# Sixty tasks of a written-out order moved ahead of the key sums, and four halves of query features swapped between VectorE and GpSimd

## The chip, the cores and the metric

The kernel runs on one core of a Trainium2 chip. The time is the device time of one execution in microseconds (us), and the median of the runs is what counts. A profiled execution has its own time and a span, from its first to its last instruction; the places below are given in us from the start of that span.

## The reference

The input x has 2048 tokens of 512 features. A small network on a vector c gives six vectors of 512 (shift, scale and gate for each of two branches). The first branch is linear attention with 32 heads of 16 features, the second a gated feed-forward network of width 1376:

```python
mod = (_silu(c) @ w_mod).reshape(c.shape[0], 6, 1, -1)
h = _layernorm(x) * (1 + ca) + sa
qkv = h @ wqkv                       # q, k, v per head
pq, pk = q @ w_phi, k @ w_phi        # per head, 16 x 16
phi_q = concat([softmax(pq), softmax(-pq)]); phi_k likewise
kv = einsum('bhsf,bhsd->bhfd', phi_k, v);  z = sum of phi_k over s
o = (phi_q . kv) / (phi_q . z + 1e-6)
x = x + ga * (o @ wo)
h = _layernorm(x) * (1 + cb) + sb
x = x + gb * ((sigmoid(h @ w_gate) * (h @ w_up)) @ w_down)
```

The sums kv and z go over all 2048 tokens, so no token's attention output can be made before every token's key features are in.

## The kernel before

The tokens are 16 tiles of 128. The whole program is a graph of 1230 named tasks, each with one or a few instructions on one engine. The text `ORDER` lists the tasks in one sequence; `Graph.arrange` walks it, gives buffers out in that sequence (7 feature buffers, 8 PSUM banks and so on) and hands each task to its engine. A suffix `@A`, `@D` or `@P` puts a task on ScalarE (ACT), VectorE (DVE) or GpSimd (POOL) instead of its first choice. No scheduler follows: each engine runs its tasks strictly in the order of the text, and waits where an input is not there. SyncE (SP) issues nearly all transfers, also in the order of the text, and they all go to one DMA queue, q1.

The names that matter here:

- `ld_...`: loads. `ld_wmga` (512 KB, line 555) and `ld_wmm2` (1536 KB, line 556) are parts of w_mod, `ld_wo` (512 KB, line 557) is the output projection.
- `wqT0` to `wqT3` (line 669): the query weights, transposed by DMA from DRAM into `wT_sb`, 128 KB each. The key weights are loaded as they are and transposed on TensorE (`tpw`, `wTc`).
- `fold0k` (line 679): four matmuls on TensorE (PE) that multiply block k of the transposed query weights by w_phi; `foldc0k` (line 685) copies the product to `wqk_f`. `fold1k` and `foldc1k` do the same for the keys.
- `st1_`, `rs1_`, `nmr1_`, `xn1_`: the first layernorm. `tph`, `hm1_`: its result transposed and modulated into `h1T`. For tiles 10 to 13 the transposition is a DMA, `xT1_` (line 736).
- `Kt`, `Vt`, `Qt` (lines 817, 821, 871): four matmuls of 512 columns each. `K` gives feature inputs of the keys, `V` the values, `Q` feature inputs of the queries. `Qt` needs all four `foldc0k`.
- `et`, `nt`, `rt`, `phit`: exponentials (ACT), their sums (DVE), the reciprocals and the products for the keys; `va` copies the values; `kvt` (line 282) adds a tile into the sums. `qet`, `qnt`, `qphit.0` and `qphit.1`, `pTt`: the same for the queries, with a DMA transposition at the end.
- `modca`, `modc2` (line 616): 16 and 48 matmuls of one column for the modulation, from `ld_wmga` and `ld_wmm2`.
- `kvn`, `kvz`: the finished sums, masked, into `kvb`. From there on the order has attention outputs (`num`, `out`), the second layernorm and the feed-forward network (`g`, `u`, `y`).

```python
G.add(f"fold{side}{kt_in}", {"PE": 0.24}, f3, r=[("wT", side, kt_in), "bd"], w=[("fold", side, kt_in)], bufs=[ps])
G.add(f"Q{t}", {"PE": 0.87}, f_q, r=h1k + [("wqk", j, 0) for j in range(KT)], w=[("qk", t)], bufs=[qp])
```

Of the kernel before, what the change touches and what calls it, by code (L numbers as in the profile page):

```python
# [15 lines left out]
P = 128  # L16
S, D, H, DH, F = 2048, 512, 32, 16, 1376
# [30 lines left out]
r2.0@A va1 va2@D r3.0@A Q0 st1_13 rs1_7@P hm1_82@A n1.0 hm1_42@A kv0.0 Q2 Q1 r1.0@A phi3.0@D phi2.0@D modc2.0 qe0.0 modc2.1 nmr1_7 qe2.0 ld_wo xn1_12 phi1.0@D
tph51 qe1.0 modc2c xn1_13 qn0.0 e4.0 kv1.0 qn2.0 hm1_52 kv2.0 Q4 K5a kv3.0 xT1_12 xT1_13 qphi0.0@P qphi0.1@P qn1.0 qe4.0 qphi2.1 tph80 K5b hm1_80@A hm1_51@A
e5.0 pT0 qphi2.0 n4.0 r4.0@A qn4.0 n5.0 phi4.0@D qphi1.1@P hm1_61@P qphi1.0@P tph53 V5 K7a V4 va5 hm1_53@A V6 pT2 hm1_70@P qphi4.1 va4 hm1_71 mask4 va6 K6a  # L50
K7b K6b e6.0 K8 tph83 hm1_83 r5.0 qphi4.0@P e8.0 pT1 pT4 ld_wd2 tph81 hm1_81 n6.0 n8.0 e7.0 n7.0 V7 kv4.0 hm1_72@P K11 K9 V9 K14 V8 r6.0@A e9.0 va7 va9 r7.0@A
e11.2 e11.6 phi5.0 phi6.0 hm1_73@P n9.0 r9.0@A kv5.0 gwa gra gwb e11.4 e14.0 K10 phi7.0@D kv6.0 K12 V10 kv7.0 e14.4 r8.0 n11.6 n11.2 r11.6 phi9.0 e10.0 e12.0
ld_wd ld_wu0 grb n11.4 n14.0 r11.2 n14.4 r14.0 n10.0 r14.4@A phi8.0 va8 V11 V14 n12.0 e11.0 K13 n11.0 phi11.6 r11.4 wo1 r11.0 va10 r10.0@A va11 kv8.0 kv9.0
phi11.2@D phi11.0@D phi10.0@D phi11.4@D V12 K15 e13.0 wmod_free ld_wg0 phi14.4 phi14.0 kv10.0 kv11.4 kv11.6 Q6 kv11.0 e13.4 r12.0@A e15.4 n13.0 n13.4 r13.0
r13.4 n15.4 e15.0 va14 V15 V13 qe6.0 va12 kv11.2 n15.0 r15.0 r15.4@A va13 phi13.4 Q5 phi15.4 phi13.0@D va15 phi15.0@D phi12.0@D wo0 wo3 Q3 kv12.0 kv13.0
kv14.0 kv15.0 qn6.0 kvn0 kvz0 kv13.4 kv14.4 kv15.4 kvz1 kvn1 num0a num1a num2a wo2 rd0a wo_all rd1a qe3.0 u0a num0b num4a num1b rd0b Q11 qe5.0 rd2a u0b u2a
rd4a num2b qn3.0 u1a rd1b tpo0 Q8 qphi6.0@P qphi6.1@P oT0 out0 num4b rd2b u1b wd0 qe11.0 u2b qphi3.1@P qphi3.0@P x1_0 rd4b st2_0 qe8.0 Q7 qe7.0 tpo1 oT1 Q10
Q9 out1 Q15 oT2 rs2_0 qn5.0 nmr2_0 xn2_0 u4a u4b x1_1 qn7.0 tsw xnT0 out2 qphi5.1@P qphi5.0@P pT6 mod02 mod00 qphi7.0@P pT3 mod03@A mod01@A qe15.0 qphi7.1@P
Q13 g0.8 x1_2 tg0.8 g0.1 st2_1 wd1 rs2_1 tg0.1 u0.8 u0.1 g0.0 num3b g0.4 hm0.1 hm0.8 pT5 qe9.0 tg0.4 g0.9 wd2 u0.4 u0.9 rd3b u3b tg0.9 g0.5 num3a hm0.4 hm0.9
u0.2 u0.0 num6a tg0.5 tg0.0 rd3a u3a u0.5 g0.2 hm0.0 hm0.5 rd6a nmr2_1 qe10.0 tg0.2 oT4 g0.10 u0.10 wd6 hm0.2 g0.3 pT7 tg0.3 u6a g0.6 num6b u0.3 y0.0 y0.1  # L60
rd6b tg0.10 hm0.10 hm0.3 num5a num5b u6b rd5b wd3 wd4 wd5 oT3 oT6 xn2_1 qe13.0 tg0.6 rd5a y0.2 u5b g0.7 tg0.7 out4 u5a oT5 qn11.0 u0.6 u0.7 xnT1 num7a hm0.6
hm0.7 mod13@A mod12@A rd7a x1_4 y0.3 out3 qphi11.1@P qphi11.0@P x1_3 st2_3 out6 mod10@A mod11@A g1.2 tg1.2 g1.1 tg1.1 num7b wd7 u1.3 u1.2 hm1.2 u7a g1.4 u1.1
y0.4 rd7b hm1.1 u1.4 y0.5 tg1.4 hm1.4 g1.0 g1.10 u1.10 g1.3 u7b st2_2 rs2_2 tg1.10 tg1.3 hm1.10 hm1.3 pT11 out5 tg1.0 u1.7 g1.7 x1_6 nmr2_2 u1.0 hm1.0 g1.5
# [995 lines left out]
```

## Time and profile before

| | |
|---|---|
| median of 3 runs | 204.66 us (203.75 to 204.67) |
| the profiled execution's own time | 204.01 us |
| its span | 202.3 us |
| PE busy | 195.3 us (97%) |
| DVE / ACT / POOL busy | 160.1 / 105.1 / 104.7 us |
| key sums masked (kvn, kvz) | at 56.8 to 57.7 us |
| bytes moved by DMA | 22.92 MB |

In a timeline row the first number is the start in us, the second how long the merged instructions took from the first one's start to the last one's end. A row's matmuls overlap with those of the next row, so that the distance from start to start tells the pace of PE. What stands in brackets is idle time ahead of the row and what ended it. The granted TensorE clock of the whole span is 1.00.

### The profile page before, as it was taken

The page shows a single profiled execution, that of the slowest core. Times are in us where ns is not written, and L with a number is a line of the kernel's source. Part 1 is how long each engine was busy: PE and PEld are TensorE (multiplying, and loading weights), DVE is VectorE, ACT ScalarE, POOL GpSimd, SP SyncE. Part 2 cuts the span into 40 slices and gives each one's busy share as a digit, 9 for nine tenths or more (in the row PEclk, how much of TensorE's full clock was granted, in tenths as well). Part 3 has the DMA queues.
Part 4 walks back from the last instruction along what each step waited for, and adds up shares of the span by engine and source line. Part 5 has one row for each costly group of instructions (what it writes and reads, how often), then busy time and mean ns, then how long its engine had stood idle before and what let it go on. Part 6 is the DMA issues. An engine that isn't in the chain of part 4 may idle for free.

```text
span 202.3 us, 4156 instructions
## 1 busy us (share of the span) xinstructions
PE 195.3 (97%) x1471; PEld 106.1 (52%) x1471; DVE 160.1 (79%) x374; ACT 105.1 (52%) x253; POOL 104.7 (52%) x147
## 2 busy tenths in 40 slices
PE   7989999999999999999999999999999999999993
PEld 2555565455464787668844444444444444444442
DVE  3999989999999999998897796884969754326623
ACT  2899998999978985576441215212113320334100
POOL 4999987888699998866670066130030332000000
PEclk9999999999999999999999999999999999999999
DMA  5999956669973963418655233542113031000011
GB/s 169 326 293 236 282 213 122 111 57 241 393 281 74 136 103 59 80 34 102 129 78 80 54 76 82 104 105 52 26 26 81 2 78 52 30 3 20 33 55 55
DMA packets 49452, 22.92 MB, mean 113 GB/s; under 512 B 38065, under 2 KB 47634, under 8 KB 49426
## 3 DMA queue, kind: packets, MB, share of 16 engines
q1 hardware_dynamic: 48896, 22.59, 49.7%
q8 instruction: 12, 0.20, 0.4%
q14 instruction: 14, 0.11, 0.2%
q10 hardware_dynamic: 530, 0.02, 0.1%
HBM read 11.58 MB, written 2.10 MB: 68 GB/s over the span
## 4 chain that ended last, share of the span: by engine, by line
PE 74%; DVE 7%; DMA 6%; ACT 5%; SPq 3%; issue 2%; POOL 1%; POOLq 0%; DVEq 0%; ACTq 0%
PE y_ps L485 19%; PE u_ps L447 18%; PE g_ps L447 17%; DMA wmod_sb<-in_w_mod_dram 6%; PE a_ps L356 6%; PE k_ps L817 3%; PE v_ps L821 3%; PE num L326 2%; PE q_ps L871 2%; ACT e L776 2%; DVE ks L780 2%; PE g_ps L449 1%; DVE qks L780 1%; SPq L537 1%; DVE phi L787 1%
## 5 line engine op out<-in xcount | busy, mean ns | idle before, releaser
L457 ACT ACTIVATE tg<-g_ps 128x512 bf16<-128x512 f32 (+5 forms) x66 | 28.9, 455 | 66.8 <-PE g_ps L447 39.7
L485 PE MATMUL y_ps<-wd_sb,wmod_sb 128*128 128x512 bf16 (+4 forms) x187 | 45.7, 367 | 0.0
L468 DVE SCALAR_TENSOR_TENSOR wmod_sb<-tg,u_ps 128x512 bf16<-128x512 bf16 (+4 forms) x63 | 30.3, 491 | 18.0 <-ACT tg L457 11.5
L447 PEld LDWEIGHTS <-wg_sb 128*128 128x128 bf16 (+1 forms) x252 | 21.9, 99 | 16.1
L447 PEld LDWEIGHTS <-wu_sb 128*128 128x128 bf16 (+1 forms) x252 | 21.8, 99 | 15.9 <-issue 0.3
L784 POOL TENSOR_TENSOR qphi<-qe,qks 128x512 bf16<-128x512 bf16 x24 | 25.1, 1061 | 4.2 <-DMA pT<-qphi 1.6
L485 PEld LDWEIGHTS <-wmod_sb 128*128 128x128 bf16 (+1 forms) x187 | 17.0, 97 | 16.0 <-issue 0.6
L447 PE MATMUL u_ps<-wT_sb,wu_sb 128*128 128x512 bf16 (+2 forms) x124 | 23.8, 322 | 0.0
L447 PE MATMUL g_ps<-wT_sb,wg_sb 128*128 128x512 bf16 (+2 forms) x124 | 23.1, 322 | 0.0
L447 PE MATMUL g_ps<-wqk_sb,wg_sb 128*128 128x128 bf16 (+4 forms) x128 | 20.0, 287 | 0.0
L447 PE MATMUL u_ps<-wqk_sb,wu_sb 128*128 128x128 bf16 (+4 forms) x128 | 19.8, 287 | 0.1
L376 POOL TENSOR_SCALAR ve<-mv 128x2 f32<-128x2 f32 (+1 forms) x8 | 1.8, 224 | 33.7 <-DVE mv L366 33.6
L492 DVE TENSOR_TENSOR ot<-y_ps,x 128x512 bf16<-128x512 f32 (+2 forms) x17 | 11.1, 654 | 10.2 <-PE y_ps L485 10.1
L780 DVE TENSOR_REDUCE qks<-qe 128x64 bf16<-128x1024 bf16 x16 | 19.2, 1204 | 0.0
L780 DVE TENSOR_REDUCE ks<-e 128x64 f32<-128x1024 bf16 (+2 forms) x22 | 19.1, 899 | 0.0
L776 ACT ACTIVATE e<-k_ps 128x512 bf16<-128x512 f32 (+2 forms) x44 | 18.0, 514 | 0.0
L776 ACT ACTIVATE qe<-q_ps 128x512 bf16<-128x512 f32 x32 | 17.1, 613 | 0.6 <-POOL phi L787 0.3
L817 PE MATMUL k_ps<-wqk_f,h1T 128*128 128x512 bf16 x64 | 16.6, 379 | 0.0
L871 PE MATMUL q_ps<-wqk_f,h1T 128*128 128x512 bf16 x64 | 15.9, 378 | 0.4 <-ACT wqk_f L685 0.4
L356 PE MATMUL a_ps<-wo_sb,oT 128*128 128x512 bf16 x64 | 16.3, 379 | 0.0
L787 POOL TENSOR_TENSOR phi<-e,kr 128x1024 bf16<-128x1024 bf16 (+2 forms) x10 | 14.4, 1446 | 3.3 <-ACT kr L795 2.1
L821 PE MATMUL v_ps<-wv_sb,h1T 128*128 128x512 bf16 x64 | 15.8, 379 | 0.2 <-ACT vaug L836 0.2
(132 smaller groups left out, 307.4 us busy)
## 6 DMA issues: line engine op xcount, KB each, us to landing
out_dram<-ot SPq DMA_DIRECT2D x15, 128.0 KB, 1.8
x_sb<-in_A_x_dram SPq DMA_DIRECT2D x6, 256.0 KB, 4.7
wmod_sb<-in_w_mod_dram SPq DMA_DIRECT2D x1, 1536.0 KB, 6.9
wu_sb<-in_B_w_up_dram SPq DMA_DIRECT2D x1, 1376.0 KB, 11.3
wg_sb<-in_B_w_gate_dram SPq DMA_DIRECT2D x1, 1376.0 KB, 12.1
wd_sb<-in_B_w_down_dram SPq DMA_DIRECT2D x1, 1280.0 KB, 8.3
wmod_sb<-in_w_mod_dram SPq DMA_DIRECT2D x4, 256.0 KB, 6.1
wqk_sb<-in_A_wqkv_dram SPq DMA_DIRECT2D x2, 256.0 KB, 4.4
```

The costliest lines, as they stand in the source:

```text
L356: pe.matmul(ap_[:], lhsT=oT[:, j, :], rhs=wo_sb[:, j, :], start=(j == 0), stop=(j == KT - 1))
L447: pe.matmul(ps[:fsz, 0:n], lhsT=w[:, j, ft * P:ft * P + fsz], rhs=h[:, j, 0:n], start=(j == 0), stop=(j == KT - 1))
L457: G.add(f"tg{k}.{ft}", {"ACT": 0.13 + n * 0.00083}, lambda e, tg=tg, g_ps=g_ps, fsz=fsz, n=n: act.activation(tg[:fsz, 0:n], g_ps[:fsz, 0:n ...
L468: dve.scalar_tensor_tensor(hm_all[:fsz, hm[k].slot, ft, 0:n], tg[:fsz, 0:n], 1.0, u_ps[:fsz, 0:n], op0=ALU.add, op1=ALU.mult)
L485: mm = pe.matmul(y[:, 0:c1 - c0], lhsT=hm_all[:fsz, hm[k].slot, ft, tl * P:(tl + 1) * P], rhs=wd_sb[:fsz, ft, c0:c1], start=(ft == 0), sto ...
L776: act.activation(ee[:, a:b, s].rearrange("p g f h -> p g (f h)"), kp[:, a * 64:b * 64].rearrange("p (g n) -> p g n", n=64), ACT.Exp, scale ...
L780: dve.tensor_reduce(ks[:, a:b].rearrange("p g s h -> p (g s) h"), ee[:, a:b].rearrange("p g s f h -> p (g s) h f"), axis=AX.X, op=ALU.add)
L784: engine(e).tensor_tensor(ph[:].rearrange("p (g s f h) -> p g s f h", s=2, f=DH, h=4)[:, :, s], ee[:, :, s], ks[:, :, 1 - s].unsqueeze(2). ...
L787: engine(e).tensor_tensor(ph[:, a * P:b * P].rearrange("p (g f h) -> p g f h", f=DH, h=4), ee[:, a:b].rearrange("p g s f h -> p (g s) f h" ...
L817: pe.matmul(kp[:], lhsT=h1T[:, j, t * P:(t + 1) * P], rhs=wqk_f[:, j, D:2 * D], start=(j == 0), stop=(j == KT - 1))
L821: pe.matmul(vp[:], lhsT=h1T[:, j, t * P:(t + 1) * P], rhs=wv_sb[:, j, :], start=(j == 0), stop=(j == KT - 1))
L871: pe.matmul(qp[:], lhsT=h1T[:, j, t * P:(t + 1) * P], rhs=wqk_f[:, j, 0:D], start=(j == 0), stop=(j == KT - 1))
```

## The change

Only the text `ORDER` differs, in its first third (words 10 to 378 of 1230). No task is added or taken away; some sixty stand at another place, and four go to another engine: `qphi1.0` and `qphi1.1` from POOL to DVE, `qphi2.0` and `qphi4.1` from DVE to POOL. From the key sums on, the two texts are the same. A replay of measured times of the tasks gave the new sequence.

The places in order of the program:

- `ld_wk1` is issued ahead of `ld_wk0`, `tpw3` runs ahead of `tpw1`, `fold11` after `tpw2` and a warm-up matmul, and `tph13` after the second half of the first modulation.
- `ld_wmm2` and `ld_wo` are issued right after `ld_wmga`, ahead of `wqT0` and the `xT1_` transpositions.
- `fold00` and `foldc00` stand right after `tph50` (before: after `V1` and half of `K4`).
- The queries of tiles 0, 1, 4 and then 2 are made in that sequence (before: 0, 2, 1 and 4), with their exponentials, sums and features.
- `xn1_8`, `st1_8`, `st1_13`, `hm1_62`, `hm1_52`, `hm1_71`, `tph53`, `V4`, `V13`, `K14`, `va7`, `ld_wd2`, `gwa`, `wo1` and a few more stand some places earlier or later.

Two stretches of the text, cut to the places:

```diff
-rs1_5@P K0b ld_wv0 wqT3 tph30 tph33 tph32 K2a tph42 hm1_40 wqT2 fold01 hm1_33 tph31 nmr1_6 K2b ld_wmga st1_14 hm1_30@A xn1_11 e0.0 hm1_31@A wqT0 xn1_10 xT1_11
+rs1_5@P K0b ld_wv0 wqT3 tph30 tph33 tph32 K2a tph42 hm1_40 wqT2 fold01 hm1_33 tph31 nmr1_6 K2b ld_wmga ld_wmm2 st1_14 ld_wo hm1_30@A xn1_11 e0.0 hm1_31@A wqT0
...
-modca.0 va0 foldc02 modca.1 tph50 n2.0 xn1_15 modcac hm1_50 n3.0 e1.0 xn1_14 phi0.0 hm1_60@P V1a V1b hm1_62@P K4a hm1_63@P fold00 tph82 tph52 K4b foldc00
+hm1_32 modca.0 va0 foldc02 modca.1 tph50 n2.0 fold00 foldc00 xn1_15 modcac hm1_50 n3.0 e1.0 xn1_14 phi0.0 hm1_60@P V1a V1b st1_13 K4a hm1_63@P tph82 tph52 K4b
```

On SP the transfers around 15 us of the trace stood in this order before (`wqk_sb` from w_mod is `ld_wmga`, `wmod_sb` with 1536 columns is `ld_wmm2`, the first `wT_sb` row here holds `wqT3` and `wqT2`, the second `wqT0`):

```order
L669 DMA_TRANSPOSE wT_sb<-in_A_wqkv_dram 128x4x128 x2
L555 DMA wqk_sb<-in_w_mod_dram 128x4x512
L669 DMA_TRANSPOSE wT_sb<-in_A_wqkv_dram 128x4x128
L736 DMA_TRANSPOSE h1T<-xn 128x4x128 x2
L556 DMA wmod_sb<-in_w_mod_dram 128x4x1536
L557 DMA wo_sb<-in_A_wo_dram 128x4x512
L736 DMA_TRANSPOSE h1T<-xn 128x4x128 x2
```

and now in this one:

```order
L669 DMA_TRANSPOSE wT_sb<-in_A_wqkv_dram 128x4x128 x2
L555 DMA wqk_sb<-in_w_mod_dram 128x4x512
L556 DMA wmod_sb<-in_w_mod_dram 128x4x1536
L557 DMA wo_sb<-in_A_wo_dram 128x4x512
L669 DMA_TRANSPOSE wT_sb<-in_A_wqkv_dram 128x4x128
L736 DMA_TRANSPOSE h1T<-xn 128x4x128 x4
```

The two loads of 2 MB together, which stood behind `wqT0` and two `xT1_`, now stand ahead of them.

On PE the four matmuls of `fold00` come in ahead of `V1` (the row above them is the end of `tph50`, the rows below the start of `V1`), and are taken out further down, between the two halves of `K4`:

```order
 L744 LDWEIGHTS xn
 L744 MATMUL tp_h<-ident,xn 128x128
+L679 LDWEIGHTS wT_sb
+L679 MATMUL fold_ps<-bd,wT_sb 128x128
+L679 LDWEIGHTS wT_sb
+L679 MATMUL fold_ps<-bd,wT_sb 128x128
+L679 LDWEIGHTS wT_sb
+L679 MATMUL fold_ps<-bd,wT_sb 128x128
+L679 LDWEIGHTS wT_sb
+L679 MATMUL fold_ps<-bd,wT_sb 128x128
 L821 LDWEIGHTS h1T
 L821 MATMUL v_ps<-wv_sb,h1T 128x512
```

So `fold00` runs about 1.3 us of matmuls earlier in PE's queue, and `V1`, `K4` and the queries stand behind it.

On ACT the copy of `fold00` (line 685) moves the same way, ahead of the copy for the modulation and the exponentials of key tile 1:

```order
 L836 CAST vaug_111<-v_ps 128x32x16
-L685 CAST wqk_f<-fold_ps 128x512
+L685 CAST wqk_f<-fold_ps 128x512 x2
 L648 COPY gcol<-modc_ps 128x4
 L776 ACTIVATE e<-k_ps 128x8x64 x2
-L685 CAST wqk_f<-fold_ps 128x512
 L794 ACTIVATE ks<-ks 128x64
 L795 ACTIVATE kr<-ks 128x64
```

The exponentials, which stood ahead of the copy, now stand behind it.

More of the change, by code (lines that the diff above doesn't have):

```diff
@@ L48 @@
[L48 to L51, printed above, removed]
@@ new lines @@
+rs1_5@P K0b ld_wv0 wqT3 tph30 tph33 tph32 K2a tph42 hm1_40 wqT2 fold01 hm1_33 tph31 nmr1_6 K2b ld_wmga ld_wmm2 st1_14 ld_wo hm1_30@A xn1_11 e0.0 hm1_31@A wqT0
+xn1_10 xT1_11 K3a xT1_10 K3b foldc01 nmr1_5 V3a st1_15 e3.0 V0a rs1_8@P e2.0 xn1_8 V0b V3b fold03 va3 foldc03 V2a st1_12 n0.0 V2b xn1_9 fold02 nmr1_8 r0.0@A
+hm1_32 modca.0 va0 foldc02 modca.1 tph50 n2.0 fold00 foldc00 xn1_15 modcac hm1_50 n3.0 e1.0 xn1_14 phi0.0 hm1_60@P V1a V1b st1_13 K4a hm1_63@P tph82 tph52 K4b
+r2.0@A va1 va2@D r3.0@A Q0 rs1_7@P hm1_82@A Q1 n1.0 hm1_42@A kv0.0 Q4 r1.0@A phi3.0@D phi2.0@D modc2.0 qe0.0 modc2.1 hm1_52 nmr1_7 xn1_13 qe1.0 xn1_12
@@ new lines @@
+phi1.0@D tph51 xT1_13 qe4.0 modc2c tph53 qn0.0 e4.0 kv1.0 qn1.0 kv2.0 Q2 kv3.0 xT1_12 qphi0.0@P qphi0.1@P K5a qn4.0 qe2.0 qphi1.1 tph80 hm1_80@A hm1_51@A K5b
+e5.0 pT0 qphi1.0 n4.0 hm1_71 r4.0@A qn2.0 n5.0 V4 phi4.0@D qphi4.1@P V5 hm1_61@P qphi4.0@P K7a hm1_53@A va5 V6 pT1 hm1_70@P gwa qphi2.1 va4 mask4 va6 K6a K7b
+K6b e6.0 K8 tph83 hm1_83 r5.0 qphi2.0@P e8.0 pT4 pT2 tph81 hm1_81 n6.0 n8.0 e7.0 kv4.0 n7.0 V7 K9 V9 V8 va7 r6.0@A hm1_62@P K11 e9.0 va9 r7.0@A e11.2 e11.6
+phi5.0 hm1_72@P phi6.0 hm1_73@P n9.0 r9.0@A kv5.0 gra gwb e11.4 K14 e14.0 K10 phi7.0@D kv6.0 K12 V10 e14.4 ld_wd2 r8.0 n11.6 n11.2 r11.6 phi9.0 e10.0 e12.0
```

80 lines of the change are left out of this document (39 added, 41 removed).

## The prediction

> **What bounds the kernel now.** I first read the page (span, busy shares), then busy time by stage, then PE's and SP's timelines at the places that the change touches.
>
> ```profile
> span 202.3 us, 4156 instructions
> PE 195.3 (97%) x1471; PEld 106.1 (52%) x1471; DVE 160.1 (79%) x374; ACT 105.1 (52%) x253; POOL 104.7 (52%) x147
> ```
>
> ```profile
> 21.00:28.00 7.00, 6.50 (x78) 3.71 (x76) 6.37 (x11) 6.81 (x21) 6.88 (x9) 1.00 1.12 321
> 28.00:57.50 29.50, 28.97 (x271) 15.73 (x269) 29.36 (x56) 28.19 (x81) 23.86 (x22) 1.00 0.75 185
> 70.00:189.00 119.00, 119.00 (x798) 64.20 (x794) 89.91 (x213) 42.16 (x92) 44.32 (x62) 1.00 0.35 63
> ```
>
> In a row of this table stand the stretch and its length, then the busy time of PE, PE's weight loads, DVE, ACT and POOL, the granted clock, the DMA share and GB/s. PE sets the end. From 70 to 189 us it never rests, and up to the key sums (57.5) it rests for 0.5 us in the stretch 21 to 28 and for another 0.5 in the 29.5 us after it. DVE is just as full there (29.36 of 29.50), ACT nearly so. The change leaves PE the same matmuls, and from the key sums on the same order. So a gain can only come out of PE's few pauses ahead of the key sums, and any new pause of PE there lasts to the end, but for what such a later pause takes up again. Here is PE around the place where most of the change lies:
>
> ```profile
> 21.49 0.27 PE L744 MATMUL tp_h<-ident,xn 128*128 128x128 bf16 x2
> 21.60 1.02 PE L821 MATMUL v_ps<-wv_sb,h1T 128*128 128x512 bf16 x4
> 22.46 0.59 PE L817 MATMUL k_ps<-wqk_f,h1T 128*128 128x512 bf16 x2
> 22.89 0.39 PE L679 MATMUL fold_ps<-bd,wT_sb 128*128 128x128 bf16 x4
> 23.11 0.39 PE L744 MATMUL tp_h<-ident,xn 128*128 128x128 bf16 x4
> 23.34 0.59 PE L817 MATMUL k_ps<-wqk_f,h1T 128*128 128x512 bf16 x2
> 24.30 1.02 PE L871 MATMUL q_ps<-wqk_f,h1T 128*128 128x512 bf16 x4 [0.36 <-ACT wqk_f L685]
> 25.16 0.42 PE L282 MATMUL kvacc<-vaug,phi 128*128 128x68 bf16 x8
> 25.41 1.89 PE L871 MATMUL q_ps<-wqk_f,h1T 128*128 128x512 bf16 x8
> 27.43 1.49 PE L616 MATMUL modc_ps<-sc_bf,wmod_sb 128*128 128x1 bf16 x48
> 28.78 0.27 PE L744 MATMUL tp_h<-ident,xn 128*128 128x128 bf16 x2
> 28.99 0.68 PE L282 MATMUL kvacc<-vaug,phi 128*128 128x68 bf16 x16
> ```
>
> Two pauses are to be seen. `K4`'s second half takes 0.43 by start-to-start pace (22.46 to 22.89), so it is through at 23.77, and `Q0` starts at 24.30: 0.53 for the copy of `fold00`. The eight query matmuls from 25.41 take 1.72 (twice the 0.86 from 24.30 to 25.16), and `modc2` starts at 27.43, not 27.13: 0.30 for `ld_wmm2`. The change takes aim at both, by an earlier `fold00` and an earlier `ld_wmm2`. What it does to the transfers in between decides.
>
> **The transfers: what is late next.** SP's issues and, from the DMA view of the stretches 14:15, 15:17, 17.9:20 and 29:32, the times from issue to landing:
>
> ```profile
> 14.44 0.58 SPq L555 DMA_DIRECT2D wqk_sb<-in_w_mod_dram  x1
> 15.06 1.57 SPq L669 DMA_TRANSPOSE wT_sb<-in_A_wqkv_dram  x1
> 17.96 2.50 SPq L736 DMA_TRANSPOSE h1T<-xn  x2
> 20.52 0.74 SPq L556 DMA_DIRECT2D wmod_sb<-in_w_mod_dram  x1
> ```
>
> ```profile
> wqk_sb<-in_w_mod_dram SPq DMA_DIRECT2D x1, 512.0 KB, 6.4
> ...
> wT_sb<-in_A_wqkv_dram SPq DMA_TRANSPOSE x1, 7.0
> ...
> h1T<-xn SPq DMA_TRANSPOSE x2, 4.2
> ...
> h1T<-xn SPq DMA_TRANSPOSE x2, 2.4
> ```
>
> `wqT0`, issued at 15.06, lands at 22.1, 7.0 later. Two transpositions of the same 128 KB, issued after 29 us when the line is empty, need 2.4. The other 4.6 it spends behind earlier transfers: `ld_wmga`, issued 0.62 ahead of it, lands at 20.8, and `wqT0` 1.2 after that; the pair issued at 17.96, behind both, needs 4.2. Each lands in the order of issue. I read this as one line in which a transposition does not overtake a load. Before the change, `fold00` at 22.89 thus came 0.8 after its data.
>
> In the new order `ld_wmm2` and `ld_wo`, 1536 + 512 KB or 2.10 MB, stand between `ld_wmga` and `wqT0`. They may be issued from 15 us on, far earlier than the line gets to them, so they follow at once. What they take:
>
> ```profile
> 21.00:22.00 1.00, 1.00 (x23) 0.79 (x21) 1.00 (x2) 0.97 (x4) 1.00 (x3) 1.00 1.57 65
> ...
> 23.00:28.00 5.00, 4.50 (x52) 2.42 (x50) 4.37 (x8) 4.84 (x15) 4.88 (x6) 1.00 1.01 386
> ```
>
> At the 386 GB/s at which these two loads moved from 23 to 28 us, 2.10 MB are 5.4 us, so `wqT0` lands at 22.1 + 5.4 = 27.5. In 21:22 the line all but stood still (65 GB/s, some 0.8 us lost). Where that doesn't come again, it is 26.7; where it does and the loads take 6 us, as at 350 GB/s, 28.1. I take 27.2, between the first two.
>
> **The sum.** PE reaches `fold00` right after `tph50`, where `V1` started before, at 21.60, and waits there until 27.2: 5.6 us (5.1 to 6.5). The small moves ahead of it (`tpw3`, `fold11`, `tph13`, `xn1_8`) I cost at nothing: whether PE is there 0.3 us earlier or later, it waits for the same landing, and the 5.6 us are the cover. Were the landing on time, each would count for itself, some 0.1 to 0.3 with either sign.
>
> Behind `fold00` in PE's queue stand `V1`, `K4`, two transposition groups, `Q0`, `Q1`, `kv0`, `Q4`, `modc2`, `tph51` and `tph53`, and then `kv1`. By the starts above: 0.22 + 0.86 + 0.43 + 0.23 + 0.43 + 0.86 + 0.86 + 0.25 + 0.86 + 1.35 + 0.11 + 0.11 = 6.57. The two old pauses are not in it; the early `fold00` and `ld_wmm2` take them away. `kv1` starts at 27.2 + 6.57 = 33.8, where it was 28.99. Of these 4.8 us, 0.1 (`tph53`) is work taken from later on: 4.7 late.
>
> The other engines wait with it, since each runs in order:
>
> ```profile
> 22.66 1.11 ACT L776 ACTIVATE e<-k_ps 128x512 bf16<-128x512 f32 x2
> 23.62 0.62 ACT L685 CAST wqk_f<-fold_ps 128x512 bf16<-128x512 f32 x1
> 26.91 3.02 ACT L776 ACTIVATE qe<-q_ps 128x512 bf16<-128x512 f32 x6
> ```
>
> ```profile
> 25.01 1.19 DVE L780 TENSOR_REDUCE ks<-e 128x64 f32<-128x1024 bf16 x1
> 26.11 1.29 DVE L787 TENSOR_TENSOR phi<-e,kr 128x1024 bf16<-128x1024 bf16 x2
> ```
>
> ACT holds `foldc00` where it waits for `fold00` (done at 27.4), and behind it the work that ran from 22.66 to 26.91 (4.25 us with the copy). It gets to `qe0` at 27.4 + 4.25 = 31.7, 4.8 late. DVE's `n1` waits for the exponentials (0.96) behind the copy (0.62) and starts at 29.0 instead of 25.01, 4.0 late. POOL waits too (last rival), and had 5.6 us of rest from 28 to 57.5 (23.86 of 29.50). So all are late by about as much as PE, and none by more.
>
> What comes back later:
>
> ```profile
> 36.89 0.39 PE L744 MATMUL tp_h<-ident,xn 128*128 128x128 bf16 x4
> 37.45 1.02 PE L821 MATMUL v_ps<-wv_sb,h1T 128*128 128x512 bf16 x4 [0.17 <-ACT vaug L836]
> ```
>
> Four transpositions take 0.22 (22.89 to 23.11 for four of the same size), so PE paused 0.34 ahead of 37.45, for ACT. ACT has a rest of 0.5 near 34 us in the stretch above (28.19 of 29.50) and can catch up by that much. I take 0.3 and another 0.1 back: PE is 4.3 late at the key sums. From there on the order is the same and PE full, so this stays. The feature halves swapped between DVE and POOL (two each way) cancel. The moves behind `kv1` (`V4`, `V13`, `K14`, `hm1_62` and the like) change places within full queues, and on SP `gwa` goes ahead of two `pT` and `ld_wd2` behind `gwb`, for users beyond 50 us; I cost both at nothing, and at 0.3 of either sign where the order of ACT's and PE's waits comes out otherwise.
>
> Then PE's pace after a rest of 5.6 us. At the program's start it was this:
>
> ```profile
> 1.25 2.74 PE L600 MATMUL warm<-wd_sb 128*128 128x512 bf16 x6 [1.25 <-DVE wd_sb L593]
> ...
> 4.11 2.10 PE L600 MATMUL warm<-wd_sb 128*128 128x512 bf16 x5
> ...
> 16.64 1.46 PE L817 MATMUL k_ps<-wqk_f,h1T 128*128 128x512 bf16 x6
> ```
>
> The first six matmuls of 512 columns took 2.74, six of the same size later 1.46: about half pace until some 5.8 us. With the five from 4.11 (2.10, against five sixths of 1.46) that cost 1.3 + 0.9 = 2.1 us. The pauses quoted above, up to 0.53, left the pace as it was (0.86 for `Q0` right after one). A restart after 5.6 us thus costs between 0 and 2.1. Ten times as long as a harmless pause, it is nearest to the only long rest in the trace, that ahead of the first matmul, and I take 2.1.
>
> The Trainium skill ("TensorE: Matmul & The Clock Gate", What's actually happening) says that the clock falls to half once a free-running window of 3.4 us passes idle, and comes back after a busy one. By this rule an idle 5.6 us would hold a whole window in about two of three cases, an estimate from that page; the half pace at the start agrees, a fall in mid-run no row here shows.
>
> Sum, against the profiled execution's own time: 204.0 + 4.3 + 2.1 = **210.4 us**. That execution stands 0.65 under the median of the runs and inside their spread (203.75 to 204.67); I leave the number as it is.
>
> **The rivals.**
>
> *PE restarts at full pace.* Everything else as above: 204.0 + 4.3 = 208.3 (207.5 to 209.0 with the landing between 26.7 and 28.1). For it: the granted clock is 1.00 in all stretches of the table. Against it: the slow start.
>
> *A transposition overtakes the loads* (the one that is not slower). If `wqT0` got through beside `ld_wmm2`, it would land by 22.1 at the latest. Then PE waits 0.45 at `fold00` (21.60 to 22.05), saves 0.53 + 0.30, and the time is 204.0 - 0.4 = 203.6; with the small moves, 203 to 204. It decides once the landing is before 22.4. For it speaks only that the three quantities are of different kinds, big loads and a transposition; against it the 7.0 and 4.2 us, where 2.4 are enough.
>
> *The line to POOL becomes the bound.* POOL's `hm1_60`, `hm1_63` and `rs1_7` follow the `xT1_` transpositions, which are next in line after `wqT0`:
>
> ```profile
> 24.54 1.63 POOL L753 TENSOR_SCALAR h1T<-h1T,modc 128x256 bf16<-128x256 bf16 x3
> 26.14 0.73 POOL L712 TENSOR_SCALAR ve<-mv 128x2 f32<-128x2 f32 x1
> 26.96 1.01 POOL L713 TENSOR_TENSOR rs<-ve,mhalf 128x2 f32<-128x2 f32 x1
> ```
>
> With 1 us for the two transfers, POOL starts at 28.2 and needs two thirds of 1.63 and 1.8 (26.14 to 27.97): `rs1_7` is there at 31.1. DVE wants it, ahead of `phi1`, after `n1` (1.1), `phi3` and `phi2` (1.3) and a piece of `h1T` (0.3), at 29.0 + 2.7 = 31.7. The margin is 0.6. A standstill of the line as in 21:22 between `wqT0` and `xT1_10` eats it; at 2 us DVE is 1.4 later and so are the key sums: 211.8 (211 to 212.5).
>
> **How the numbers follow.** 0.54 for the forecast, 0.32 for the full pace, 0.08 for the overtaking transposition, 0.06 for POOL. The forecast's own range is 209.2 to 211.9 (landing 26.7 to 28.1, and 0.5 for the restart each way). With the full pace taken in, 207.3 to 211.9. A measurement of this kernel can tell about 0.5% (1 us) from no change. Slower by over that: 0.54 + 0.32 + 0.06, less a little for surprises, 0.89. The overtaking case splits into 0.07 for no change and, if the small moves help too, 0.04 for faster.
>
> **What would show it.** In the profile after: an idle of 5 to 6.5 us on PE ahead of `fold_ps` (line 679), ended by the DMA of `wT_sb`, starting near 21.6; a `wT_sb` transposition with about 11 us from issue to landing; `modc2` and `Q0` without their pauses; all engines quiet from 25 to 27; matmuls of 512 columns 0.43 apart after 27 for some 4 us (or 0.215, then the first rival); the masked sums near 63. I am wrong if the fourth `wT_sb` lands before 23, if PE pauses there less than 3 us, or if the key sums come less than 3 us later than before.

## The result and the profile after

The change makes the kernel slower: 211.55 us (median; 210.67 to 211.72) against 204.39 us for the kernel before on the same chip, a ratio of 1.035 with a 95% interval of 1.032 to 1.038. The profiled execution took 211.54 us, 7.5 more than that of before (204.01). All of this is in the span, 209.8 against 202.3. First the page: the span, and the busy time, share and instructions of each engine.

```profile
span 209.8 us, 4135 instructions
PE 195.2 (93%) x1447; PEld 107.0 (51%) x1471; DVE 161.2 (77%) x374; ACT 105.5 (50%) x253; POOL 104.2 (50%) x147
```

PE is busy as long as before (195.2 against 195.3; of the same 1471 matmuls this trace holds 1447 records, so its sum is a little low), in a span that is 7.5 longer. Here is PE's timeline from the place of the first `fold` groups to `kv1`, and the first masked sums:

```profile
21.60 0.27 PE L744 MATMUL tp_h<-ident,xn 128*128 128x128 bf16 x2
27.53 0.61 PE L679 MATMUL fold_ps<-bd,wT_sb 128*128 128x128 bf16 x4 [5.66 <-DMA wT_sb<-in_A_wqkv_dram]
27.93 1.91 PE L821 MATMUL v_ps<-wv_sb,h1T 128*128 128x512 bf16 x4
29.64 1.06 PE L817 MATMUL k_ps<-wqk_f,h1T 128*128 128x512 bf16 x2
31.75 1.89 PE L871 MATMUL q_ps<-wqk_f,h1T 128*128 128x512 bf16 x8
33.48 0.42 PE L282 MATMUL kvacc<-vaug,phi 128*128 128x68 bf16 x8
34.59 1.48 PE L616 MATMUL modc_ps<-sc_bf,wmod_sb 128*128 128x1 bf16 x48
36.15 0.67 PE L282 MATMUL kvacc<-vaug,phi 128*128 128x68 bf16 x16
...
64.16 0.93 PE L326 MATMUL num<-kvb,pT 128*128 128x68 bf16 x24 [0.38 <-DVE kvb L299]
```

One rest of 5.66 us ahead of `fold00`, ended by `wqT0`; then the four matmuls of `V1` take 1.71 to the next row, 0.43 each, and the eight queries from 31.75 run at 0.215 again. The pauses ahead of `Q0` and `modc2` are gone. The masked sums start at 64.16 instead of 57.51, 6.65 later. From there to the end of the span it is 145.6 us, where it was 144.8.

The DMA view of the stretch 16 to 17.5 (time from issue to landing), and busy times by stage as in the prediction's table:

```profile
wT_sb<-in_A_wqkv_dram SPq DMA_TRANSPOSE x1, 10.8
```

```profile
24.00:28.00 4.00, 0.47 (x5) 0.47 (x6) 0.99 (x3) 0.00 (x0) 0.65 (x1) 0.61 1.23 236
28.00:30.00 2.00, 2.00 (x7) 0.67 (x5) 0.15 (x1) 1.80 (x6) 1.39 (x4) 0.50 0.01 4
30.00:32.00 2.00, 2.00 (x10) 1.00 (x9) 1.88 (x3) 1.97 (x7) 0.60 (x1) 0.57 0.00 0
32.00:34.00 2.00, 2.00 (x17) 1.05 (x17) 1.72 (x6) 1.63 (x6) 0.75 (x1) 1.00 0.05 12
```

`wqT0` takes 10.8 us instead of 7.0. From 24 to 28 hardly an engine works. The clock (the column after POOL's) was at half for 3.12 us of the first stretch (0.39 x 2 x 4), all of the second and 1.72 of the third: 6.84 us. The waits of the other engines from 28 to 60 us:

```profile
ACT wqk_f L685 <- PE fold_ps L679: 5.3, 1, 5.3
DVE ks L780 <- ACT e L776: 4.8, 1, 4.8
POOL h1T L753 <- DMA h1T<-xn: 3.9, 1, 3.9
```

And a pause that the kernel before does not have, 32 us behind the start of the masked sums (PE, then POOL):

```profile
96.05 0.60 PE L447 MATMUL g_ps<-wqk_sb,wg_sb 128*128 128x256 bf16 x4 [0.38 <-POOL wqk_sb L424]
```

```profile
94.91 1.10 POOL L424 TENSOR_SCALAR wqk_sb<-wqk_sb,modc 128x256 bf16<-128x256 bf16 x2 [2.23 <-DMA wqk_sb<-xn]
```

### The profile page after: what moved, and what is told of

It is laid out like the page before. It is cut to its first block, busy times and chain, and to the rows that moved or that the text cites. A ratio compares the mean times of both kernels' runs of the same rounds, so it can differ in the third digit from the quotient of the medians.

```text
span 209.8 us, 4135 instructions
## 1 busy us (share of the span) xinstructions
PE 195.2 (93%) x1447; PEld 107.0 (51%) x1471; DVE 161.2 (77%) x374; ACT 105.5 (50%) x253; POOL 104.2 (50%) x147
## 4 chain that ended last, share of the span: by engine, by line
PE 63%; DVE 8%; SPq 7%; DMA 6%; ACT 6%; POOL 4%; issue 3%; POOLq 0%; ACTq 0%; DVEq 0%
PE y_ps L485 17%; PE u_ps L447 16%; PE g_ps L447 16%; DMA wT_sb<-in_A_wqkv_dram 5%; PE a_ps L356 4%; ACT e L776 2%; SPq L669 2%; PE num L326 2%; PE q_ps L871 2%; POOL phi L787 2%; SPq L537 2%; DVE qks L780 2%; DVE ks L780 2%; SPq L542 2%; DMA wqk_sb<-xn 1%
## 5 line engine op out<-in xcount | busy, mean ns | idle before, releaser
L485 PE MATMUL y_ps<-wd_sb,wmod_sb 128*128 128x512 bf16 (+4 forms) x180 | 44.2, 366 | 0.2
L817 PE MATMUL k_ps<-wqk_f,h1T 128*128 128x512 bf16 x63 | 17.2, 394 | 0.0
L821 PE MATMUL v_ps<-wv_sb,h1T 128*128 128x512 bf16 x61 | 16.3, 395 | 0.1
## 6 DMA issues: line engine op xcount, KB each, us to landing
wu_sb<-in_B_w_up_dram SPq DMA_DIRECT2D x1, 1376.0 KB, 10.3
```

The lines of the kernel that those rows point to most:

```text
L485: mm = pe.matmul(y[:, 0:c1 - c0], lhsT=hm_all[:fsz, hm[k].slot, ft, tl * P:(tl + 1) * P], rhs=wd_sb[:fsz, ft, c0:c1], start=(ft == 0), sto ...
L817: pe.matmul(kp[:], lhsT=h1T[:, j, t * P:(t + 1) * P], rhs=wqk_f[:, j, D:2 * D], start=(j == 0), stop=(j == KT - 1))
L821: pe.matmul(vp[:], lhsT=h1T[:, j, t * P:(t + 1) * P], rhs=wv_sb[:, j, :], start=(j == 0), stop=(j == KT - 1))
```

## The experiments

Twelve kernels, each beside the kernel before on the same chip (medians of before from 203.79 to 204.23). Diffs show words of `ORDER`. "Key sums" stands for the start of the first masked `num` row.

### The two loads, alone and away

`e1_loads_back` is the change without the early loads:

```diff
-... K2b ld_wmga ld_wmm2 st1_14 ld_wo hm1_30@A xn1_11 ... wqT0 xn1_10 xT1_11 K3a xT1_10 K3b
+... K2b ld_wmga st1_14 hm1_30@A xn1_11 ... wqT0 xn1_10 xT1_11 K3a xT1_10 ld_wmm2 ld_wo K3b
```

> The changed order with one thing undone: ld_wmm2 and ld_wo stand behind wqT0 and the first two xT1 transpositions again, as before the change. Theory (one transfer line; all that the change costs is wqT0 behind 2.1 MB): wqT0 lands near 22.1 again, PE waits 0.5 us or less at fold00, no restart at half pace, ratio to the kernel before 0.995 to 1.005. Rival (the other moves of the sixty cost on their own): ratio over 1.01, with new pauses of PE elsewhere ahead of the key sums.

Measured: 204.77 us, ratio 1.005 (1.002 to 1.009). Of the 7.2 us some 6 hang on the place of the loads; the rest of the change costs 0.5%.

`e2_loads_only` is the kernel before with both loads ahead of `wqT0`, `e5_wmm2_only` with `ld_wmm2` alone there:

```diff
-... K2b ld_wmga st1_14 ... wqT0 ...
+... K2b ld_wmga ld_wmm2 ld_wo st1_14 ... wqT0 ...      (e2)
+... K2b ld_wmga ld_wmm2 st1_14 ... wqT0 ...            (e5)
```

> The order before the change with one thing changed: ld_wmm2 and ld_wo stand right behind ld_wmga, ahead of wqT0. Theory: wqT0 lands near 27.5 as in the changed kernel; PE comes to fold00 later than there (22.9, after V1 and half of K4), so it waits 4.6 us, and by the queue behind fold00 is 3.4 to 3.7 late at the key sums, plus up to 2.1 if it restarts at half pace: 207.7 to 210.2, ratio 1.017 to 1.03. Rival (the early fold00 or another move is to blame): ratio 0.99 to 1.005.

> The order before the change with ld_wmm2 alone (1.57 MB) moved behind ld_wmga, ahead of wqT0; ld_wo stays behind the first two xT1. Theory (the wait goes by the bytes ahead): wqT0 lands 1.4 us earlier than with both loads, near 26.1, PE waits 3.2 us at fold00 and is 2.0 to 2.4 late at the key sums; a rest of 3.2 us may or may not bring half pace (0 to 2.1): 206.3 to 208.9. Rival (it is the number of transfers ahead or something else, not their bytes): as with both loads.

Measured: e2 209.15 us, ratio 1.024 (1.019 to 1.029); e5 206.89 us, ratio 1.014 (1.010 to 1.019). PE ahead of `fold00` and the stage behind it, e2 first, then e5:

```profile
27.64 0.61 PE L679 MATMUL fold_ps<-bd,wT_sb 128*128 128x128 bf16 x4 [4.53 <-DMA wT_sb<-in_A_wqkv_dram]
...
63.29 0.93 PE L326 MATMUL num<-kvb,pT 128*128 128x68 bf16 x24 [0.36 <-DVE kvb L299]
```

```profile
28.00:30.00 2.00, 2.00 (x11) 1.07 (x9) 0.00 (x0) 1.66 (x6) 1.36 (x3) 0.50 0.02 4
```

```profile
26.40 0.40 PE L679 MATMUL fold_ps<-bd,wT_sb 128*128 128x128 bf16 x4 [2.99 <-DMA wT_sb<-in_A_wqkv_dram]
```

```profile
28.00:30.00 2.00, 2.00 (x18) 1.04 (x16) 1.19 (x2) 1.88 (x7) 1.92 (x5) 1.00 0.14 43
```

`wqT0` lands behind whatever stands ahead of it: PE resumes at 27.6 behind two loads and at 26.4 behind one. In these two profiled executions a rest of 4.53 is followed by half pace and one of 2.99 is not (one of e5's four runs has a mean clock of 0.992 all the same, and so have some runs of the kernel before). So e5 loses about what PE rests (2.9 us by the ratio), and e2 4.9 us for 4.53.

The changed kernel's wait is longer than e2's since its `fold00` stands ahead of `V1` and half of `K4`. `e12_fold00_late` puts `fold00` and `foldc00` alone back behind these:

```diff
-... tph50 n2.0 fold00 foldc00 xn1_15 ... V1a V1b st1_13 K4a hm1_63@P tph82 tph52 K4b r2.0@A ...
+... tph50 n2.0 xn1_15 ... V1a V1b st1_13 K4a fold00 hm1_63@P tph82 tph52 K4b foldc00 r2.0@A ...
```

> The changed kernel with fold00 and foldc00 alone back behind V1 and the first half of K4, the loads early as in the change. Theory: the transposition lands at the same time (28.0), V1 and half of K4 (about 1.3 us) now lie in the wait, so that PE rests 4.4 instead of 5.7 us and all is 0.8 to 1.3 earlier: 210.2 to 210.9 against 211.55. Rival (the end does not go by PE's rest there, but by the line or by the engines behind it): 211.2 to 211.9.

Measured: 210.49 us, ratio 1.032 (1.026 to 1.038), as the theory had it, though this interval overlaps that of the change.

```profile
28.13 0.43 PE L679 MATMUL fold_ps<-bd,wT_sb 128*128 128x128 bf16 x4 [4.33 <-DMA wT_sb<-in_A_wqkv_dram]
...
63.11 0.93 PE L326 MATMUL num<-kvb,pT 128*128 128x68 bf16 x24 [0.38 <-DVE kvb L299]
```

PE rests 1.3 less and the key sums come 1.05 earlier. Its four runs also price the half pace: two have a mean granted clock of 0.992 (one stretch of 3.4 us at half) and took 209.48 and 210.17; two have 0.984 (two such stretches) and took 210.81 and 211.62, 1.4 more on average. That is a rough price from two runs each: in e2 three runs at 0.992 took 208.3 to 209.53, and the one at 0.984 took 209.57, 0.7 more than their mean. The changed kernel has two such stretches in each of its six runs (0.982 to 0.984).

### The half pace taken away

The pause was filled with matmuls on a constant tile, whose results are overwritten, so that the clock does not fall. The first, `e4_filled_pause`, used a PSUM buffer of its own, which shifted the turn of the eight banks; `e6` (on e2) and `e7` (on the change) use the bank of `fold00`. In e4 it is 25 matmuls, in e6 18, in e7 22:

```diff
+G.add("fill00", {"PE": 4.3}, lambda e, ps=ps: [pe.matmul(ps[:], lhsT=wd_sb[:, FT - 1, 0:P],
+      rhs=wd_sb[:, FT - 1, :], start=True, stop=True) for _ in range(18)], r=["c1"], w=["warm"], bufs=[ps])
-... K4a hm1_63@P fold00 ...
+... K4a hm1_63@P fill00 fold00 ...
```

> The changed order, with 25 more warm-up matmuls (512 columns, 5.4 us at full pace, results unused) on PE right ahead of fold00, inside its wait for wqT0. Theory (the rest lets PE's pace fall to half, which costs about 2 us): fold00 starts at the same time as in the changed kernel, all matmuls behind it run 0.215 apart, and the time is 1.5 to 2.2 us under that of the changed kernel (211.5): 209.3 to 210.0, mean clock 1.00. Rival (the slow matmuls lie beside waits for ACT and DVE and cost nothing): 211 to 212.

> The kernel before with the two loads early (the run e2), and 18 idle matmuls of 512 columns (3.9 us) in the bank of fold00 itself, right ahead of it in PE's queue; no other buffer changes its turn, and what they compute is overwritten by fold00. Restart theory (after a rest of 4.7 us PE runs at half pace for 6.8 us, which costs about 2 us): wqT0 lands near 28.0 as in e2, PE rests under 1 us, the clock stays at full and the time is 206.9 to 207.4 against 209.15 of e2. Rival (the line and the other engines set the key sums or what follows them, and the half pace is hidden behind them): 208.7 to 209.6.

> The changed kernel with 22 idle matmuls of 512 columns (4.7 us) in the bank of fold00 itself, so that the turn of the PSUM banks stays that of the changed kernel (in the run e4 it did not). Theory that e4's loss after the key sums came from its shifted banks: the price of the restart comes off to the end, 209.2 to 210.0. Rival that the transfers behind the key sums (the last weights, pT and oT on the one line) do not get earlier with PE: key sums 1.5 to 2 us earlier than in the changed kernel, as in e4, but pauses of PE of 2 us or more between 70 and 97 us, and 211.3 to 212.5.

Measured: e4 212.3 us, ratio 1.039 (1.035 to 1.044); e6 209.08 us, ratio 1.024 (1.020 to 1.028); e7 210.56 us, ratio 1.031 (1.027 to 1.036). The expectation of the restart theory failed in e4 and e6, and e7 lies between the two theories: two of its runs (209.83 and 209.94) fall where the restart theory had them and two (211.18 and 211.46, the latter at a clock of 0.989) by the lower end of the rival. The profiled one, 211.18, came late to the pause already: its `fold00` starts at 28.70, 1.2 later than in the change, as SP's issues are 1.1 to 1.3 later from 6.6 us on. Yet up to the key sums the theory holds. PE in e6 and in e7:

```profile
27.87 0.40 PE L679 MATMUL fold_ps<-bd,wT_sb 128*128 128x128 bf16 x4 [0.66 <-DMA wT_sb<-in_A_wqkv_dram]
...
61.86 0.93 PE L326 MATMUL num<-kvb,pT 128*128 128x68 bf16 x24 [0.36 <-DVE kvb L299]
74.05 0.30 PE L326 MATMUL num<-kvb,pT 128*128 128x68 bf16 x4 [0.29 <-DMA pT<-qphi]
```

```profile
28.70 0.40 PE L679 MATMUL fold_ps<-bd,wT_sb 128*128 128x128 bf16 x4 [0.77 <-DMA wT_sb<-in_A_wqkv_dram]
...
63.29 0.93 PE L326 MATMUL num<-kvb,pT 128*128 128x68 bf16 x24 [0.38 <-DVE kvb L299]
```

From `fold00` to the key sums it is 35.65 us in e2 and 33.99 in e6, 36.63 in the change and 34.59 in e7: the half pace costs 1.7 and 2.0 there. But from the key sums to the end e6 takes 145.7 us against 144.5 of e2, and gives back 1.2. The row at 74.05 says where the first part goes: PE waits for a transposition `pT`. Counted from the key sums and set against e2, PE is 0.46 late from that row on, 0.76 from 75.23 on, where it also waits for ACT's `qe`, and 1.16 from 155.04 on. The DMA view of the transfer of `pT` (issued 7.7 us behind the key sums in both), e2 first, then e6, and last what else moved in e6 from 71 to 72.5 us:

```profile
pT<-qphi SPq DMA_TRANSPOSE x1, 3.1
```

```profile
pT<-qphi SPq DMA_TRANSPOSE x1, 4.4
```

```profile
q1 hardware_dynamic: 849, 0.21, 75.5%
q8 instruction: 1, 0.02, 4.2%
```

One packet of queue 8, kind "instruction", of 16 KB and 1.0 us, lies in the middle of the transposition's 256-byte packets. At 155.04 it is the same again: PE waits for a transposition `oT` that takes 4.2 us from issue to landing in e6 and 2.4 in e2, and a 16 KB packet starts at 152.63 in e6, where e2 has it at 158.44. The traces have 12 or 13 such packets per execution (13 in e6), in step with PE's progress. Here is where the one of this stage starts (from the packets' records, set to the timeline's zero; the 10.3 and 12.7 in the expectation of e10 below were read without that), with the instructions that a fill adds to PE:

```
kernel   added to PE   key sums   16 KB packet    behind them   key sums to end
before        0          57.51       70.00           12.5            144.8
e2            0          63.29       75.65           12.4            144.5
e6           36          61.86       71.69            9.8            145.7
change        0          64.16       76.50           12.3            145.6
e12           0          63.11       75.57           12.5            145.3
e7           44          63.29       72.91            9.6            146.1
e4           50          62.56       72.60           10.0            148.9
```

In e4 a second packet falls onto a transposition `oT`, for which PE waits 1.31; whether that, or its shifted banks, makes it lose more than e7 was not settled. So a probe that adds PE instructions shifts PE's instruction transfers against the work, and here onto a transposition that PE waits for. The Trainium skill ("DMA: Bandwidth & Descriptors", Queues, rings and completion order) says that each DMA engine takes turns between its queues, a whole packet at a time; the 1.0 us of one 16 KB packet, and the 1.3 us more of the transposition, agree; the 1.8 more of `oT` is longer than its packet of 0.93 us, which that rule alone does not give. `e10` and `e11` repeat e6 and e7 with exactly 128 matmuls and 128 weight loads, mostly of one column:

```diff
-      ... rhs=wd_sb[:, FT - 1, :] ... for _ in range(18)]
+      ... ps[:, 0:c] ... rhs=wd_sb[:, FT - 1, 0:c] ... for i in range(128) for c in [512 if i % 25 == 0 and i < 125 else 1]]
```

> Like e6 (the kernel before with the two loads early, PE kept busy ahead of fold00), but the fill is 128 matmuls with their weight loads, 5 of 512 columns and 123 of one column, about 4.5 us by the 28 ns of such a matmul in modc2. In the trace PE's instructions come in by transfers of 16 KB; in e6, with 36 instructions more than in e2, they come some 2.4 us earlier against the key sums (10.3 us behind them instead of 12.7), fall on the transposition pT that PE waits for next, and e6 gives back 1.2 of the 1.4 us after the key sums. If 16 KB are 256 instructions, 128 pairs shift them by one whole transfer and they fall where they do in e2. Theory of the shifted fetch: key sums near 61.9 as in e6 if the clock holds, no pause of 0.46 near 74, after the key sums 144.5 to 144.9 us instead of 145.7, 207.3 to 208.2. Rival (other engines or the line are what is late after the key sums, whatever the fetch): as e6, 208.7 to 209.6. If the clock falls in spite of the narrow matmuls: 209 to 209.5, and the question stays open.

> The changed kernel with the same kind of fill (9 matmuls of 512 columns and 119 of one column, some 5.3 us, 256 PE instructions). Theory of the shifted fetch: the price of the half pace comes off to the end, 209.0 to 210.0 against 211.55 of the changed kernel and 210.56 of e7. Rival: as e7, 210.3 to 211.3.

Measured: e10 209.95 us, ratio 1.030 (1.026 to 1.034); e11 210.06 us, ratio 1.030 (1.025 to 1.034). In both the packet is back at its place, 12.4 us behind the key sums, and from these to the end it is 144.6 us in e10 and 145.1 in e11, 1.0 to 1.1 less than in e6 and e7: this part of the theory held. In e11 the gain reaches the end, 0.5% or 1.1 us by the ratios (the intervals overlap). In e10 it does not, for another reason:

```profile
34.73 0.68 PE L282 MATMUL kvacc<-vaug,phi 128*128 128x68 bf16 x16 [1.52 <-DVE phi L787]
...
63.24 0.93 PE L326 MATMUL num<-kvb,pT 128*128 128x68 bf16 x24 [0.36 <-DVE kvb L299]
```

Its key sums are no earlier than e2's, since `kv1` waits 1.52 for `phi1`, behind POOL, whose `h1T` waited 5.54 for the `xT1_` transpositions. An instruction packet at 27.5 lies next to these, and POOL goes on 1.2 later than in e6. In e11 it is the same (a packet at 27.3, POOL's wait 5.36 against 3.88 in the change), but there no `kv1` waits for it. Besides, in three of e10's four runs the mean clock is 0.981 to 0.992. No trace shows where it fell in these, so that the narrow matmuls let it fall is not shown; two of the seven runs of the kernel before on this chip have 0.992 too. So e10's time decides nothing about the price of the half pace, as its expectation had allowed for.

### The small moves

`e8` puts `ld_wmm2` right behind `wqT0`, `e9` moves only `fold00` and `foldc00` forward (both from the kernel before), and `e13` is the kernel before up to `tph50` and the change's sequence from there on, with the loads behind the `xT1_`:

```diff
-... wqT0 xn1_10 xT1_11 K3a xT1_10 ... foldc03 ld_wmm2 V2a ...
+... wqT0 ld_wmm2 xn1_10 xT1_11 K3a xT1_10 ... foldc03 V2a ...      (e8)
-... tph50 n2.0 xn1_15 ... K4a hm1_63@P fold00 tph82 tph52 K4b foldc00 ...
+... tph50 fold00 foldc00 n2.0 xn1_15 ... K4a hm1_63@P tph82 tph52 K4b ...      (e9)
```

> The kernel before with ld_wmm2 right behind wqT0, that is ahead of xT1_11 and xT1_10 and not ahead of wqT0. Theory that what hurts is wqT0 alone: wqT0 lands at 22 to 22.5, the pause ahead of modc2 (0.30) goes, 203.3 to 204.0 where before has 203.8 on the last chip. Rival that the line to POOL decides (xT1_11 and xT1_10 land near 27 instead of 23, hm1_60, hm1_63, rs1_7 and nmr1_7 follow): key sums 0.5 to 2 us later, 204.5 to 206.

> The kernel before with fold00 and foldc00 alone moved right behind tph50, the loads where they were. Theory: wqT0 lands at 22.1, PE rests 0.45 there, the 0.53 ahead of Q0 goes: 203.6 to 204.0 (0 to 0.3 less than before). Rival: the copy ahead of the exponentials of key tile 1 holds ACT until 22.4 and DVE behind it, 204.2 to 204.8.

> The kernel before up to tph50, and from there on the sequence of the change, with both loads behind the xT1_ transpositions (ld_wo right behind ld_wmm2). So of the change only the moves behind tph50 are in: fold00 and foldc00 early, the queries in the sequence 0, 1, 4, 2, the four swapped halves, gwa, ld_wd2 and the rest. Kernels with the change's sequence have a pause of 0.3 to 0.4 us of PE ahead of g_ps (line 447) at 12 to 33 us behind the key sums' start, ended by wqk_sb from POOL, and kernels with the sequence of before do not. Theory that the early moves (ahead of wqT0) cost the other part of the 0.5% of e1, by pauses that let the clock fall in the opening: here the opening is that of before, the clock stays at full, the pause ahead of g_ps remains, 0.3 to 0.6 us above before, 204.1 to 204.5 where before has 203.8. Rival (the moves behind tph50 carry it all): 204.6 to 205.2, ratio 1.004 to 1.007. Rival that they gain and the early moves lose: below 203.6, no pause ahead of g_ps.

Measured: e8 206.99 us, ratio 1.015 (1.011 to 1.019), more than even its rival had; e9 203.96 us, ratio 0.999 (0.996 to 1.001); e13 204.38 us, ratio 1.002 (1.000 to 1.005). The two runs of e8 with a clock of 0.998 and 1.0 took 205.9 and 206.24, about the upper end of what its rival had; the other four have 0.983 to 0.992 and took 206.65 to 208.31. So a slower clock is part of this median, in a place that no trace shows. The profiled execution is the one of 206.24. PE, DVE and POOL in it:

```profile
31.24 0.68 PE L282 MATMUL kvacc<-vaug,phi 128*128 128x68 bf16 x16 [1.85 <-DVE phi L787]
```

```profile
30.25 0.34 DVE L718 TENSOR_SCALAR nmr<-mv,rs 128x1 f32<-128x1 f32 x2 [2.44 <-POOL rs L713]
```

```profile
26.90 2.33 POOL L753 TENSOR_SCALAR h1T<-h1T,modc 128x256 bf16<-128x256 bf16 x3 [1.91 <-DMA h1T<-xn]
```

`wqT0` is on time there, and the loss comes by the line to POOL: `xT1_` late, `hm1_60` on POOL late, `rs1_7` late, DVE waits 2.44 for it in `nmr1_7` ahead of `phi1`, and PE 1.85 for that. This is the chain of the prediction's last rival, with PE on time. In e9 the early `fold00` only shifts pauses:

```profile
22.18 0.40 PE L679 MATMUL fold_ps<-bd,wT_sb 128*128 128x128 bf16 x4 [0.40 <-DMA wT_sb<-in_A_wqkv_dram]
27.75 1.49 PE L616 MATMUL modc_ps<-sc_bf,wmod_sb 128*128 128x1 bf16 x48 [0.37 <-DMA wmod_sb<-in_w_mod_dram]
```

What it saves ahead of `Q0` it waits at `fold00` and `modc2`. In e13 the late moves bring the pause ahead of `g_ps`, at full clock and with the opening of before:

```profile
57.62 0.93 PE L326 MATMUL num<-kvb,pT 128*128 128x68 bf16 x24 [0.36 <-DVE kvb L299]
...
89.30 0.60 PE L447 MATMUL g_ps<-wqk_sb,wg_sb 128*128 128x256 bf16 x4 [0.33 <-POOL wqk_sb L424]
```

All seven kernels with the change's sequence behind `tph50` (the change, e1, e4, e7, e11, e12, e13) have it, 0.31 to 0.42 in this column; before and the kernels with its sequence (e2, e5, e6, e8, e9, e10) do not. In all seven SP issues the second of two transpositions into `wqk_sb` 1.63 to 1.64 us behind the first, in all others 1.23; which moved task makes it so was not tried. The early moves bring something else. The six kernels that have them (the change, e1, e4, e7, e11, e12) rest 0.35 to 0.39 ahead of the second group of key weights, at 6.75 to 8.10, and no other kernel does. The rest ahead of the first group is longest in e1's profiled execution, which took 206.64 us, more than e1's median. PE, and busy times by stage:

```profile
6.99 0.40 PE L661 MATMUL tp_w<-ident,wqk_sb 128*128 128x128 bf16 x4 [1.40 <-DMA wqk_sb<-in_A_wqkv_dram]
```

```profile
4.60:8.00 3.40, 1.65 (x14) 0.75 (x13) 3.04 (x12) 1.06 (x5) 2.92 (x4) 1.00 1.04 325
8.00:11.00 3.00, 3.00 (x23) 2.18 (x21) 2.43 (x7) 2.04 (x4) 2.28 (x6) 0.50 1.18 307
```

A rest of 1.40 ahead of the key weights, and the clock at half from 8 to 11. Three of e1's twelve runs have such a mean clock (0.992) and took 206.2 to 206.6; eight with 0.997 to 1.0 took 204.4 to 204.9, and one with 1.0 took 206.8. That the early moves cause the slower clock is not shown: runs of the kernel before and one of e13 have that clock too.

## Why the prediction was right

The forecast of 210.4 us lies 1.15 below the median, inside its own range (209.2 to 211.9), and the likeliest case is the one that happened. Step by step:

- **One transfer line, and no overtaking.** Right. `wqT0` 10.8 us from issue to landing (about 11 forecast), PE resumed at 27.53 (27.2 forecast; with the standstill of the line 27.5 had been worked out, and the standstill came again: from 26 to 26.75 us the line moved 23 GB/s). e1, e2 and e5 show that the landing goes by what is ahead.
- **PE waits at `fold00`.** Idle for 5.66 us, from 21.87 to 27.53; the forecast was 5.6, from 21.60 to 27.2. e12 shows the part of it that comes from the early `fold00`.
- **`kv1`.** Forecast 33.8 at full pace, and 35.9 with the 2.1 for the restart; it started at 36.15.
- **The restart at half pace.** Right, and the assumed 2.1 is 1.7 to 2.0 up to the key sums by e6 and e7. The clock was at half for 6.84 us, of which the last 4.2 fell into PE's work. The size is partly luck: it was taken whole from the one slow start in the trace (whose rows give 1.28 + 0.88 = 2.16), and while all six runs of the change have two stretches of 3.4 us at half, three of four runs of e2, with a rest 1.1 shorter, have the mean clock of one (0.992). To the end it was worth 1.4 per 3.4 us stretch between runs of e12 and 0.7 between those of e2 (few runs each), 1.1 (for both stretches) between the change and e11, and nothing between e2 and e6, where shifted instruction packets took it back. The Trainium skill ("TensorE: Matmul & The Clock Gate", What's actually happening) has an idle window of 3.4 us for the fall; 4.33 to 5.66 us of rest lost the pace and 2.99 kept it, which agrees. But the 3.4 us right ahead of each fall were not wholly idle: PE was busy in them for 0.24 us in e12, 0.39 in the change, 0.80 in e2 and 1.65 in e1, where the rest was only 1.40; and in e5 a stretch of 3.4 us with 0.41 us of work (23 to 26.4) kept the pace. What decides between these is open.
- **What comes back.** 0.4 forecast; from `kv1` (7.16 late) to the key sums (6.65 late) it was 0.5.
- **The small moves cost nothing.** Mis-sized: without the early loads they cost 0.5% or 1.1 us in e1, where the text allowed 0.3 of either sign. e13 finds 0.2% of this in the moves behind `tph50`, with an interval that takes in no change.
- **"From there on the order is the same and PE full, so this stays."** Wrong by 0.85 us, most of the 1.1 that the forecast misses between the two profiled executions (the rest is 0.25 up to the key sums). The order is the same, but the state that engines and queues come with is not: at the pause ahead of `g_ps` PE's lateness behind the key sums grows from 0.16 to 0.68, 0.52 of the 0.85, and e13 shows that it goes with the moves behind `tph50`. The rest are gaps of 0.1 to 0.2 that were not followed up.
- **The base.** 204.0 of the profiled execution; the median of before on the chip of the comparison was 204.39. Counted in medians the base is thus 0.4 too low, and the difference 7.2 instead of 7.5.
- **The bounds.** They do not follow exactly from the terms given: a landing at 26.7 to 28.1 and 0.5 each way for the restart make 209.4 to 211.8, not 209.2 to 211.9, and the first rival's landings make 207.8 to 209.2, not 207.5 to 209.0. Nothing hangs on these 0.1 to 0.3 us.

Of the rivals, the full pace fell with the clock at 0.50 in the stages above, the overtaking with the 10.8 us. The line to POOL did not decide in the changed kernel, since PE and DVE were late by more; e8 and e10 show that it decides at once when the `xT1_` are late by more than PE (`kv1` waits 1.85 and 1.52), so a margin of 0.6 is little.

None of the experiments beats the kernel before: e9 cannot be told from it.

## What to carry to other kernels

When transfers share one queue, an early issue of a big load is a delay of everything behind it: before moving a load forward, list what it passes and when each of these is needed, and in this kernel two such lists (PE's `wqT0`, POOL's `xT1_`) left no place. A pause of a full engine also has a second price, the slower clock behind it, which up to the key sums added about a third to the first (1.7 to 2.0 us behind rests of 4.5 to 5.7). And a wait should stand behind the work that doesn't need it: the same late landing cost 1.3 us more of rest because `fold00` had been moved ahead of `V1`.

## What was not expected of the hardware

- PE's instructions come in as 16 KB packets on the DMA engines during the run, 12 or 13 of them, and two that fell into DMA transpositions made them 1.3 and 1.8 us longer (4.4 against 3.1, 4.2 against 2.4). 36 to 50 added PE instructions brought the packet of one stage 2.3 to 2.7 us earlier, 256 put it back where it was. A probe or a warm-up that adds instructions thus moves times far behind it.
- Narrow matmuls can hold the full clock: 119 of one column with 9 wide ones in between did so in all four runs of e11. With 5 wide ones only one of e10's four runs stayed at 0.997, and where the others lost the clock is open.
- The clock fell behind stretches of 3.4 us in which PE had worked for 0.24 to 1.65 us, in four traces: PE need not rest for all of such a stretch to lose the pace.
